# A fused attention and feed-forward kernel: new due times, filler transposes, batch 1's q on GpSimd, a halved last step

## The chip, the cores and the metric

The kernel runs on one core of a Trainium2 chip. The metric is the device time of one execution in microseconds (us), measured on the chip; each time below is a median of several runs, or the time of one profiled run where that is said.

The engines are named as the profile names them: PE (TensorE, matrix products and transposes), PEld (its weight loads), DVE (VectorE), ACT (ScalarE), POOL (GpSimd) and SP (SyncE, which only issues transfers here).

## The reference

```python
def _attn_ref(q, k, v):                       # each 8 batches x 8 heads x 576 x 64
    q_s = q - np.max(q, axis=-1, keepdims=True)
    q_s = np.exp(q_s)
    q_s = q_s / (np.sum(q_s, axis=-1, keepdims=True) + 1e-09)
    k_s = k - np.max(k, axis=2, keepdims=True)
    k_s = np.exp(k_s)
    k_s = k_s / (np.sum(k_s, axis=2, keepdims=True) + 1e-09)
    kv = np.einsum('bhsd,bhse->bhde', k_s, v)
    return np.einsum('bhsd,bhde->bhse', q_s, kv)

def _moe_ref(x, w_in, w_out, s, b):           # x 4608x512, w_in 512x2048, w_out 2048x512
    h = x @ w_in
    r = np.maximum(h, 0.0)
    g = s * (r * r) + b
    return g @ w_out
```

x is the attention's result, transposed to (batch, position) rows by (head, d) columns. All data are float32. To keep float32's accuracy on PE's faster fp32r products, every factor of the two large products is split in a high and a low part, and each product is three matmuls: high by high, high by low, low by high.

## The kernel before

**Blocks and steps.** The 4608 rows of x are done in nine blocks of 512: the first 512 positions of each of the eight batches, and a ninth block of the 64 positions that each batch has left. The 2048 columns of w_in are 16 chunks of 128. A step t is one block and one chunk, 144 in all. Step t computes h_t with 12 matmuls (four pieces c of the 512-long contraction, each of three matmuls), each 128x512. ACT takes the relu into r (L751), DVE squares and scales it (L764), ACT adds b and rounds to the high part gh (L766), DVE subtracts to the low part gl (L768). In odd steps of block 0 ACT does the squaring and scaling instead (L755, L757, L759; DVE L761). Then 12 matmuls (four quarters j of three) add g's product with the chunk of w_out into four accumulators acc. h has one PSUM bank, so h_{t+1} can start only when relu_t has read h_t.

**Weights.** In block 0 the chunk f of both weight matrices is loaded (tile st) and split by `conv_w`: ACT L199, L202 and L220, DVE L205, L210, L212, L215 and L222. L222 writes the low part and is the last of a chunk; its result is w_f, which h_f needs.

**Attention.** A unit u is a pair of heads of one batch; a batch has four units, and pr = u // 2 is a pair of units. Batches 0 and 1 (units 0 to 7) go through `q_stream`: maxima of q (L412), subtraction (L414), exp on ACT, sums and reciprocals (L420 to L424), scaling (L426), transposes qT on PE (L430), a copy on ACT (L433), product with kv into xp (L440), and the split of xp in x's high part (ACT L446) and low part (DVE L449). xp of unit u gives piece c = u mod 4 of the block's x: h_0's last piece needs x_0's unit 3, h_16's last piece needs unit 7. `k_stream`, `k_pair`, `kv_stream` and `kv_second` make kv for these batches. In the later batches (`k_late`, `q_late`, `kv_late`, `x_late`) q's subtraction and scaling are on POOL (L575, L592), and x comes from xp and xq (L676) by way of a tile y (ACT L682, DVE L686).

**The end.** `leave` copies a finished accumulator out and stores it; `leave_last` does so for the last block. There quarters 0 and 1 are copied by ACT, quarter 2 by DVE, and quarter 3 by both, half each; each quarter is stored by two transfers, one from SP's queue and one from ACT's.

**What sets the order.** Nothing reorders at compile time: each engine runs its instructions in the order in which a planner, the class `Order`, writes them. Each stream (one unit's q, one chunk's conversion, one step ...) is a generator that yields an `Op(engine, cost, due, needs ...)` ahead of each piece of work. The planner takes, over and over, the piece that can start first by its own costs, and among those that start within NEAR of it the one with the smallest due. Due times are written by hand: the tables DUE_K, DUE_Q, DUE_V (by unit or pair) and DUE_W, and t - 1, t - 2 and t + 0.5 in the steps. TRIP and RATE are its estimate of a transfer, COLD the time until which it counts PE at half speed. In `needs`, a piece names what has to be there first; `late` adds a margin.

Of the kernel before, what the change touches and what calls it, by code (L numbers as in the profile page):

```python
# [26 lines left out]
def attention_moe(ctx: ExitStack, tc: tile.TileContext, q, k, v, w_in, w_out, s, b, out):  # L27
# [375 lines left out]
    def q_stream(u):  # L403
# [10 lines left out]
        nc.vector.tensor_tensor(out=qt, in0=qt, in1=bc(qm, [P, 2, NT, D]), op=ALU.subtract)  # L414
# [11 lines left out]
        nc.vector.tensor_tensor(out=qe, in0=qe, in1=bc(qr, [P, NT, 2, D]), op=ALU.mult)  # L426
# [231 lines left out]
    def x_late(u):  # L658
# [19 lines left out]
        for a, at in enumerate((slice(0, L), slice(L, L + M))):  # L678
            for h in range(2):
                yield Op("ACT", 0.4, due, take=() if y else ["tmp"])  # L680
                y = y or work.tile([P, 2 * L], F32, name=f"y_{u}", tag="tmp", bufs=NTMP)
                nc.scalar.copy(y[half[h], at], parts[h][a][half[1 - h]])  # L682
        for a, at in enumerate((slice(0, L), slice(L, L + M))):
            for h in range(2):
                yield Op("DVE", 0.44, due, free=["big", "sm"] if a and h else ())
# [52 lines left out]
    def step(t):  # L738
# [12 lines left out]
        nc.scalar.activation(r, hp_, AF.Relu)  # L751
# [31 lines left out]
    def o_parts(t):  # L783
# [4 lines left out]
        for j in tile_order(t):  # L788
# [3 lines left out]
            for i, (g, w_) in enumerate(((gh, w[:, 0]), (gh, w[:, 1]), (gl, w[:, 0]))):  # L792
                nc.tensor.matmul(  # L793
                    acc[blk, j // 2][:, j % 2], g[:, js], w_, start=(f == 0 and i == 0), stop=(f == NFC - 1 and i == 2)
                )
            yield
# [14 lines left out]
    def leave_last(j):  # L811

        t = NSTEP - 1

        whole, half = slice(0, DO), (slice(0, DO // 2), slice(DO // 2, DO))
        todo = [("ACT", 0.55, whole), ("ACT", 0.55, whole), ("DVE", 0.6, whole), ("ACT", 0.35, half[0])][j]
        yield Op(todo[0], todo[1], t, needs=[f"o{t} {j}"])
        a = acc[B, j // 2][:, j % 2]
        if not lasts:
            lasts.append(work.tile([P, 2 * NT * P], F32, name="last", tag="qhl"))  # L820
        o = work.tile([P, DO], F32, name=f"o_{B}_{j}", tag="qe", bufs=2) if j > 1 else lasts[0][:, j * DO:(j + 1) * DO]
        (nc.vector.tensor_copy if j == 2 else nc.scalar.copy)(o[:, todo[2]], a[:, todo[2]])  # L822
        if j == NQ - 1:
            yield Op("DVE", 0.4, t, needs=[f"o{t} {j}"])
            nc.vector.tensor_copy(o[:, half[1]], a[:, half[1]])
        for i, (e, eng) in enumerate((("SP", nc.sync), ("ACT", nc.scalar))):
            yield Op(e, 0.1, t)
            bb = 2 * j + i
            eng.dma_start(out[bb * S + TB:(bb + 1) * S, :], o[i * LEFT:(i + 1) * LEFT, :])
# [130 lines left out]
```

## Time and profile before

| | us |
|---|---|
| median of 3 runs | 875.56 |
| lowest, highest | 875.45, 876.37 |
| profiled run, its own time | 875.49 |
| span of the profile | 873.7 |
| PE busy | 850.2 |
| DVE busy | 573.0 |
| ACT busy | 411.2 |
| POOL busy | 96.0 |
| mean granted PE clock | 0.995 |

The span begins with the first instruction that the profiler shows and ends with the last; 1.8 us of the run's time lie around it. Busy times are sums over instructions, so an engine's share of the span is an average over stages in which different engines set the pace. A row of the timeline gives start, duration, engine, line, operation, result and operands; what stands in brackets behind it is the engine's idle time just before it and what ended that.

### The profile page before, as it was taken

How to read it: one execution, taken by the hardware profiler on the slowest of the kernel's cores; microseconds unless marked ns; L12 is line 12 of the kernel's file. 1: busy time of each engine (PE TensorE's matmuls, PEld its weight loads, DVE VectorE, ACT ScalarE, POOL GpSimd, SP SyncE). 2: the span in 40 equal slices, each digit the busy share in tenths (PEclk: the TensorE clock that was granted, in tenths of full speed). 3: DMA queues.
4: the chain of work that ended last, by engine and by line, in shares of the span. 5: the costliest groups of instructions: out<-in, count | busy, mean ns of one | idle time of the engine just before them, and what ended most of it. 6: DMA issues, size and time to landing. Idle time of an engine off the chain costs nothing.

```text
span 873.7 us, 11481 instructions
## 1 busy us (share of the span) xinstructions
PE 850.2 (97%) x4312; PEld 698.1 (80%) x4312; DVE 573.0 (66%) x931; ACT 411.2 (47%) x676; POOL 96.0 (11%) x110
## 2 busy tenths in 40 slices
PE   4799999999999999999999999999999999999997
PEld 3577887888888888888888888888888888888886
DVE  6999997687887957696577748685764322232222
ACT  5898854455453544454345534444444322222222
POOL 1000002020221201220031102020200010000000
PEclk9999999999999999999999999999999999999999
DMA  9968024524444224332433242431411000000001
GB/s 241 314 249 266 6 73 117 140 80 90 135 107 128 57 73 116 111 74 64 129 88 86 84 130 72 99 88 71 98 50 51 25 25 1 0 28 22 1 0 49
DMA packets 109959, 79.44 MB, mean 91 GB/s; under 512 B 60624, under 2 KB 103632, under 8 KB 109776
## 3 DMA queue, kind: packets, MB, share of 16 engines
q1 hardware_dynamic: 108496, 77.60, 31.9%
q10 hardware_dynamic: 1408, 1.12, 0.4%
q8 instruction: 34, 0.56, 0.3%
q14 instruction: 21, 0.17, 0.1%
HBM read 60.29 MB, written 18.40 MB: 90 GB/s over the span
## 4 chain that ended last, share of the span: by engine, by line
PE 85%; DVE 5%; DMA 3%; issue 3%; ACT 2%; SPq 2%; ACTq 0%; DVEq 0%
PE h L726 41%; PE acc L793 40%; PE kv L298 2%; DMA v<-in_v_dram 1%; DMA st<-in_moe_w_out_dram 1%; DVE low L215 1%; PE xq L676 1%; PE xp L676 1%; DVE w L222 1%; DMA k<-in_k_dram 1%; DVE st L212 1%; DVE st L210 0%; DVE low L205 0%; ACT r L751 0%; PE xp L440 0%
## 5 line engine op out<-in xcount | busy, mean ns | idle before, releaser
L726 PE MATMUL h<-x,w 128*128 128x512 f32 x1728 | 421.6, 392 | 2.6 <-DVE x L449 1.0
L726 PEld LDWEIGHTS h<-x,w 128*128 128x128 f32 x1728 | 323.8, 188 | 72.2 <-DVE x L449 1.7
L793 PE MATMUL acc<-w,gh 128*128 128x512 f32 x1152 | 358.1, 392 | 0.0
L793 PEld LDWEIGHTS acc<-w,gh 128*128 128x128 f32 x1152 | 214.1, 188 | 44.6 <-ACT last L822 0.4
L764 DVE SCALAR_TENSOR_TENSOR r<-r,sb 128x512 f32<-128x512 f32 x136 | 107.7, 792 | 199.0 <-ACT r L751 198.1
L793 PE MATMUL acc<-w,gl 128*128 128x512 f32 x576 | 224.8, 390 | 0.3 <-DVE gl L768 0.3
L751 ACT ACTIVATE r<-h 128x512 f32<-128x512 f32 x144 | 85.9, 597 | 280.5 <-PE h L726 277.1
L768 DVE SCALAR_TENSOR_TENSOR gl<-r,sb,gh 128x512 fp32r<-128x512 f32 x136 | 105.0, 772 | 54.1 <-ACT gh L766 53.3
L766 ACT ACTIVATE gh<-r,sb 128x512 fp32r<-128x512 f32 x136 | 98.5, 724 | 80.5 <-DVE r L764 79.5
L793 PEld LDWEIGHTS acc<-w,gl 128*128 128x128 f32 x576 | 108.1, 188 | 24.2 <-DVE gl L768 0.9
L575 POOL TENSOR_TENSOR q<-q,qm 128x640 f32<-128x640 f32 x24 | 35.4, 1486 | 163.3 <-DVE qm L573 163.3
L592 POOL TENSOR_TENSOR qe<-qe,qr 128x640 f32<-128x640 f32 x24 | 36.6, 1527 | 45.4 <-DVE qr L588 34.7
L682 ACT COPY y<-xp 64x320 f32<-64x320 f32 x48 | 20.2, 420 | 11.7 <-PE xp L676 11.1
L298 PEld LDWEIGHTS kv<-v,k 128*64 128x64 f32 x600 | 19.8, 143 | 7.3 <-issue 4.9
L656 POOL TENSOR_TENSOR spare<-kvf,spare 128x256 fp32r<-128x256 f32 x12 | 9.3, 778 | 144.9 <-issue 137.8
L686 DVE TENSOR_TENSOR y<-xp,y 64x320 f32<-64x320 f32 x48 | 23.4, 488 | 1.4
L613 DVE TENSOR_TENSOR qhl<-qT,qhl 64x640 fp32r<-64x640 f32 x24 | 20.6, 860 | 5.2 <-ACT qhl L608 4.6
L298 PE MATMUL kv<-v,k 128*64 128x65 f32 (+1 forms) x600 | 21.9, 230 | 2.1 <-DMA v<-in_v_dram 2.1
L579 ACT ACTIVATE qe<-q 128x640 f32<-128x640 f32 x24 | 18.8, 786 | 9.1 <-POOL q L575 9.1
L690 ACT CAST x<-y 128x512 fp32r<-128x512 f32 x24 | 14.7, 614 | 15.5 <-DVE y L686 15.5
L686 DVE TENSOR_TENSOR y<-xq,y 64x256 f32<-64x256 f32 x48 | 20.2, 422 | 1.4
L562 ACT ACTIVATE k<-k 128x640 f32<-128x640 f32 x24 | 17.4, 736 | 7.3 <-DVE k L524 7.3
(121 smaller groups left out, 608.5 us busy)
## 6 DMA issues: line engine op xcount, KB each, us to landing
st<-in_moe_w_in_dram SPq DMA_DIRECT2D x16, 512.0 KB, 8.6
st<-in_moe_w_out_dram SPq DMA_DIRECT2D x16, 512.0 KB, 8.6
out_dram<-o SPq DMA_DIRECT2D x16, 512.0 KB, 2.6
turned<-q SPq DMA_DIRECT2D x24, 320.0 KB, 2.3
qT<-turned SPq DMA_DIRECT2D x48, 160.0 KB, 3.1
q<-in_q_dram SPq DMA_DIRECT2D x14, 512.0 KB, 5.3
k<-in_k_dram SPq DMA_DIRECT2D x14, 512.0 KB, 4.3
v<-in_v_dram SPq DMA_DIRECT2D x56, 128.0 KB, 4.8
```

The source lines that it names most:

```text
L298: nc.tensor.matmul(kv[h * D:(h + 1) * D, i], kt[:, i, h, n], vt[:, 2 * i + h, n], start=(n == 0), stop=(n == NT - 1))
L575: nc.gpsimd.tensor_tensor(out=qt, in0=qt, in1=bc(qm, [P, 2, NT, D]), op=ALU.subtract)
L592: nc.gpsimd.tensor_tensor(out=qe_, in0=qe_, in1=qr, op=ALU.mult)
L613: nc.vector.tensor_tensor(out=t[half[1 - h], h], in0=qT[half[h]], in1=t[half[h], h].bitcast(F32), op=ALU.subtract)
L682: nc.scalar.copy(y[half[h], at], parts[h][a][half[1 - h]])
L686: nc.vector.tensor_tensor(out=y[half[h], at], in0=parts[h][a][half[h]], in1=y[half[h], at], op=ALU.add)
L726: nc.tensor.matmul(hp_, w[:, j, c, :], x[:, c, :], start=(c == 0 and i == 0), stop=(c == NP - 1 and i == 2))
L751: nc.scalar.activation(r, hp_, AF.Relu)
L764: nc.vector.scalar_tensor_tensor(out=r, in0=r, scalar=s_col, in1=r, op0=ALU.mult, op1=ALU.mult)
L766: nc.scalar.activation(gh, r, AF.Identity, bias=b_col)
L768: nc.vector.scalar_tensor_tensor(out=gl, in0=r, scalar=b_col, in1=gh.bitcast(F32), op0=ALU.add, op1=ALU.subtract)
L793: nc.tensor.matmul(acc[blk, j // 2][:, j % 2], g[:, js], w_, start=(f == 0 and i == 0), stop=(f == NFC - 1 and i == 2))
```

## The change

Five things change.

1. All due times of batches 0 and 1 and of the first weight chunk, and the planner's constants (a transfer's TRIP 3.0 and RATE 0.315, COLD 8, PE's first piece at 3.0), and the costs that it counts for two pieces of `k_pair` and for v's load.
2. Fillers: up to h_0, where the planner sees PE idle, it puts transposes of the identity into a tile `unused` that nobody reads, which has h's bank: 26, 10, 2, 11, 10, 1 and 5 of them, 65 in all.
3. In units 4 to 7 (batch 1) the subtraction of q's maxima (L414) and the scaling (L426) go from DVE to POOL.
4. In `x_late`, the second unit of a pair also needs y of the first, with the margin WAIT; the two copies (and the two additions) to a half of y are one piece to the planner.
5. In the last step (t = 143) relu, r, gh and gl work in halves of 256 columns; the last quarter's product is two halves of three matmuls, and each half is copied and stored by itself, in four transfers in place of two.

```diff
-    DUE_K = (-30, 0.5, -20, -25, 3.5, 11.5, 12, 19.5)
-    DUE_Q = (-18, -32.5, -13.5, -6, 12.5, 9, -30.5, 64.5)
-    DUE_V = (-81.5, -28.5, -14, 31)
-    DUE_W = -15
+    DUE_K = (-41.5, -21, -37, -39.5, 4.5, 4, 12, 73.5)
+    DUE_Q = (-3.5, -35.5, -27, -7, 12.5, 3.5, -39, 78)
+    DUE_V = (-37, -28, 1.5, 15)
+    DUE_W = -28
...
-        NEAR, HOP, TRIP, RATE = 0.1, 0.15, 2.8, 0.33
-        COLD = 18
+        NEAR, HOP, TRIP, RATE = 0.1, 0.15, 3.0, 0.315
+        COLD = 8
...
+                if eng == "PE":
+
+                    self.idle(t - self.at[eng], "h" in o.take)
...
-        yield Op("DVE", 0.73, due)
-        nc.vector.tensor_tensor(out=qt, in0=qt, in1=bc(qm, [P, 2, NT, D]), op=ALU.subtract)
+        eng, cost, e = ("DVE", 0.73, nc.vector) if bb == 0 else ("POOL", 1.4, nc.gpsimd)
+        yield Op(eng, cost, due)
+        e.tensor_tensor(out=qt, in0=qt, in1=bc(qm, [P, 2, NT, D]), op=ALU.subtract)
...
-        yield Op("DVE", 0.73, due)
-        nc.vector.tensor_tensor(out=qe, in0=qe, in1=bc(qr, [P, NT, 2, D]), op=ALU.mult)
+        yield Op(eng, cost, due)
+        e.tensor_tensor(out=qe, in0=qe, in1=bc(qr, [P, NT, 2, D]), op=ALU.mult)
...
-            "PE", 0.57, due - NFC, needs=[f"q{u}", f"kvhl{pr}", f"h{NFC * (bb - 1) - 1}"], take=["big", "sm"],
+            "PE", 0.57, due - NFC, needs=[f"q{u}", f"kvhl{pr}", f"h{NFC * (bb - 1) - 1}"] + [f"y{u - 1}"] * i, take=["big", "sm"],
...
+        if t == NSTEP - 1:
+
+            halves = [slice(i * TB // 2, (i + 1) * TB // 2) for i in range(2)]
+            for i, c in enumerate(halves):
+                if i:
+                    yield Op("ACT", 0.35, t - 2, free=["h"])
+                nc.scalar.activation(r[:, c], hp_[:, c], AF.Relu)
...
+            for c in [slice(i * DO // 2, (i + 1) * DO // 2) for i in range(2)] if t == NSTEP - 1 and j == NQ - 1 else [slice(0, DO)]:
+                for i, (g, w_) in enumerate(((gh, w[:, 0]), (gh, w[:, 1]), (gl, w[:, 0]))):
+                    nc.tensor.matmul(
+                        acc[blk, j // 2][:, j % 2, c], g[:, js], w_[:, c], start=(f == 0 and i == 0),
+                        stop=(f == NFC - 1 and i == 2 and c.stop == DO)
+                    )
...
+        parts = half_ if j == NQ - 1 else [whole]
+        for k, c in enumerate(parts):
+            dve = j == 2 or k
+            yield Op("DVE" if dve else "ACT", 0.6 / len(parts), t, needs=[f"o{t} {j + k}"])
...
+            for i, (e, eng) in enumerate((("SP", nc.sync), ("ACT", nc.scalar))):
+                yield Op(e, 0.1, t)
+                bb = 2 * j + i
+                eng.dma_start(out[bb * S + TB:(bb + 1) * S, c], o[half[i], c])
...
+    unused = [ps.tile([P, 512], F32, name="unused", tag="h")]
+
+    def idle(us, last):
+        if last:
+            unused.clear()
+        for _ in range(int(0.6 * us / 0.109) if unused else 0):
+            nc.tensor.transpose(unused[0][:, 0:P], ident, ident)
```

The line numbers of the changed kernel are higher: by 3 up to `kv_stream`, by 5 from q's subtraction on, by 23 to 31 in the steps and stores.

How the order moves, at three places. In these rows stand the line, the operation, result and operands with their tile numbers, and the shape; h_16 is step 16's h, x_1 the second block's x, acc_0_0 and acc_0_2 block 0's accumulators of quarters 0, 1 and 2, 3.

PE from h_15 to h_17, before:

```order
L726 MATMUL h_15_1259<-x_0_288,w_15_1230 128x512 x12
L430 MATMUL qT_7_1279<-ident_78,qe_7_1249 128x128 x5
L726 MATMUL h_16_1290<-x_1_948,w_0_231 128x512 x9
L440 MATMUL xp_7_1306<-early_85,kvf1_84 128x256
L440 MATMUL xp_7_1306<-early_85,kvf1_84 128x320
L793 MATMUL acc_0_0_467<-w_15_1230,gh_15_1286 128x512 x2
L793 MATMUL acc_0_0_467<-w_15_1230,gl_15_1287 128x512
...
L726 MATMUL h_16_1290<-x_1_948,w_0_231 128x512 x3
L793 MATMUL acc_0_2_482<-w_15_1230,gh_15_1286 128x512 x2
L793 MATMUL acc_0_2_482<-w_15_1230,gl_15_1287 128x512
...
L726 MATMUL h_17_1347<-x_1_948,w_1_431 128x512 x12
```

The same place after the change, from the last of step 15's products:

```order
L824 MATMUL acc_0_2_549<-w_15_1257,gh_15_1300 128x512 x2
L824 MATMUL acc_0_2_549<-w_15_1257,gl_15_1301 128x512
L731 MATMUL h_16_1330<-x_1_865,w_0_277 128x512 x3
L435 MATMUL qT_7_1379<-ident_78,qe_7_1235 128x128 x5
L445 MATMUL xp_7_1388<-early_85,kvf1_84 128x256
L445 MATMUL xp_7_1388<-early_85,kvf1_84 128x320
L731 MATMUL h_16_1330<-x_1_865,w_0_277 128x512 x3
L731 MATMUL h_17_1410<-x_1_865,w_1_493 128x512 x12
```

Before, step 15's twelve products stand between xp_7 and h_17; after, they all stand ahead of qT_7, and qT_7, xp_7, the last piece of h_16 and h_17 follow each other directly. Between h_15 and these rows now stand half of step 14's products, kv_3, nine matmuls of h_16, xp_6 and step 15's products.

DVE just ahead of w_15, the last conversion (low0_15 and st_15 are its operands; q0 is batch 1's raw q, qm_7 unit 7's maxima, qe_6 unit 6's exp), before:

```order
L768 SCALAR_TENSOR_TENSOR gl_14_1159<-r_14_1157,sb_90,gh_14_1158 128x512
L426 TENSOR_TENSOR qe_6_1162<-qe_6_1162,qr_6_1182 128x640
L215 ISA low0_15_991<-st_15_883,low0_15_991 128x2048
L304 TENSOR_SCALAR z_3_1219<-kv_3_1188 128x2
L305 RECIPROCAL z_3_1219<-z_3_1219 128x2
L307 TENSOR_TENSOR zr_3_1222<-own_86,z_3_1219 128x4
L412 TENSOR_REDUCE qm_7_1228<-q0_93 128x10
L313 TENSOR_TENSOR kvf1_84<-kv_3_1188,zr_3_1222 128x256
L414 TENSOR_TENSOR q0_93<-q0_93,qm_7_1228 128x640
L222 TENSOR_TENSOR w_15_1230<-low0_15_991,w_15_1230 128x2x512
```

After, on DVE, at the same place:

```order
L425 TENSOR_REDUCE qs_6_1229<-qe_6_1220 128x10
L790 SCALAR_TENSOR_TENSOR r_14_1231<-r_14_1231,sb_90 128x512
L427 TENSOR_SCALAR qs_6_1229<-qs_6_1229 128x10
L429 RECIPROCAL qr_6_1245<-qs_6_1229 128x10
L218 ISA low0_15_1066<-st_15_965,low0_15_1066 128x2048
L794 SCALAR_TENSOR_TENSOR gl_14_1233<-r_14_1231,sb_90,gh_14_1232 128x512
L454 TENSOR_TENSOR x_1_865<-xp_4_1226,x_1_865 128x512
L225 TENSOR_TENSOR w_15_1257<-low0_15_1066,w_15_1257 128x2x512
```

And on POOL, all of batch 1's q after the change, with k's memsets between; before, POOL has only these memsets there:

```order
L419 TENSOR_TENSOR q0_93<-q0_93,qm_5_463 128x640
L431 TENSOR_TENSOR qe_5_507<-qe_5_507,qr_5_660 128x640
L490 MEMSET k0_92 64x2x64 x2
L419 TENSOR_TENSOR q0_93<-q0_93,qm_4_1105 128x640
L490 MEMSET k0_92 64x2x64 x2
L431 TENSOR_TENSOR qe_4_1128<-qe_4_1128,qr_4_1184 128x640
L419 TENSOR_TENSOR q0_93<-q0_93,qm_6_1189 128x640
L419 TENSOR_TENSOR q0_93<-q0_93,qm_7_1203 128x640
L431 TENSOR_TENSOR qe_6_1220<-qe_6_1220,qr_6_1245 128x640
L431 TENSOR_TENSOR qe_7_1235<-qe_7_1235,qr_7_1284 128x640
```

The scaling of unit 6, unit 7's subtraction and kv_3's four rows are gone from DVE ahead of w_15; on POOL stand four subtractions and, ahead of w_15, three scalings (that of unit 7 comes after it).

PE at steps 31 to 33, after the change:

```order
L731 MATMUL h_32_2182<-x_2_1749,w_0_277 128x512 x9
L824 MATMUL acc_1_0_1432<-w_15_1257,gh_31_2163 128x512 x2
L824 MATMUL acc_1_0_1432<-w_15_1257,gl_31_2164 128x512
L824 MATMUL acc_1_0_1432<-w_15_1257,gh_31_2163 128x512 x2
L824 MATMUL acc_1_0_1432<-w_15_1257,gl_31_2164 128x512
L824 MATMUL acc_1_2_1451<-w_15_1257,gh_31_2163 128x512 x2
L824 MATMUL acc_1_2_1451<-w_15_1257,gl_31_2164 128x512
L824 MATMUL acc_1_2_1451<-w_15_1257,gh_31_2163 128x512 x2
L824 MATMUL acc_1_2_1451<-w_15_1257,gl_31_2164 128x512
L731 MATMUL h_32_2182<-x_2_1749,w_0_277 128x512 x3
L731 MATMUL h_33_2240<-x_2_1749,w_1_493 128x512 x12
```

Before, all twelve matmuls of h_32 stand ahead of step 31's products; now three of them stand behind, next to h_33.

More of the change, by code (lines that the diff above doesn't have):

```diff
@@ L357, in sm @@
             return ps.tile([P, 512], F32, name=f"{n}_{pr}", tag="sm", bufs=1)
-        yield Op("DVE", 1.13, due, needs=[f"k{u} there" for u in us])
+        yield Op("DVE", 0.69, due, needs=[f"k{u} there" for u in us])
         kt = by_head(tiles[pr][0])
@@ L678, in x_late @@
         for a, at in enumerate((slice(0, L), slice(L, L + M))):
+            yield Op("ACT", (0.84, 0.74)[a], due, take=() if a else ["tmp"])
+            y = y or work.tile([P, 2 * L], F32, name=f"y_{u}", tag="tmp", bufs=NTMP)
             for h in range(2):
[L680 to L681 removed]
                 nc.scalar.copy(y[half[h], at], parts[h][a][half[1 - h]])
         for a, at in enumerate((slice(0, L), slice(L, L + M))):
+            yield Op("DVE", (0.98, 0.84)[a], due, free=["big", "sm"] if a else (), gives=[f"y{u}"] if a else ())
             for h in range(2):
[L685 removed]
                 nc.vector.tensor_tensor(out=y[half[h], at], in0=parts[h][a][half[h]], in1=y[half[h], at], op=ALU.add)
@@ L777, in step @@
             next(parts)
+            if t == NSTEP - 1 and j == NQ - 1:
+                yield Op("PE", 0.36, t + 0.5, gives=[f"o{t} {NQ}"])
+                next(parts)
     def tile_order(t):
@@ L791, in o_parts @@
             js = slice(j * P, (j + 1) * P)
[L792 to L796, printed above, removed]
+            for c in [slice(i * DO // 2, (i + 1) * DO // 2) for i in range(2)] if t == NSTEP - 1 and j == NQ - 1 else [slice(0, DO)]:
[3 more added lines that the diff above has]
+                        stop=(f == NFC - 1 and i == 2 and c.stop == DO)
+                    )
+                yield
     def leave(blk, j):
@@ L813, in leave_last @@
         t = NSTEP - 1
[L815 to L829, printed above, removed]
+        whole, half_ = slice(0, DO), (slice(0, DO // 2), slice(DO // 2, DO))
+        o = None
+        parts = half_ if j == NQ - 1 else [whole]
+        for k, c in enumerate(parts):
+            dve = j == 2 or k
+            yield Op("DVE" if dve else "ACT", 0.6 / len(parts), t, needs=[f"o{t} {j + k}"])
+            a = acc[B, j // 2][:, j % 2]
+            if not lasts:
+                lasts.append(work.tile([P, 2 * NT * P], F32, name="last", tag="qhl"))
+            if o is None:
+                o = work.tile([P, DO], F32, name=f"o_{B}_{j}", tag="qe", bufs=2) if j > 1 else lasts[0][:, j * DO:(j + 1) * DO]
+            (nc.vector.tensor_copy if dve else nc.scalar.copy)(o[:, c], a[:, c])
+            for i, (e, eng) in enumerate((("SP", nc.sync), ("ACT", nc.scalar))):
+                yield Op(e, 0.1, t)
+                bb = 2 * j + i
+                eng.dma_start(out[bb * S + TB:(bb + 1) * S, c], o[half[i], c])
     NU = B * NP
@@ L884, in v_ @@
         def v_():
-            yield Op("SP", 3.2, due, needs=[f"kv{p}"], gives=[f"v{pr} there"], kb=864)
+            yield Op("SP", 3.2, due, needs=[f"kv{p}"], gives=[f"v{pr} there"], kb=1100)
             load_v(pr)
```

29 lines of the change are left out of this document (21 added, 8 removed).

## The prediction

> **What bounds the kernel now.** I read the busy times first, then the windows by stage (in the window rows: stretch, length, busy time and instructions of PE, PEld, DVE, ACT and POOL, granted clock, DMA share, GB/s), then the waits.
>
> ```profile
> PE 850.2 (97%) x4312; PEld 698.1 (80%) x4312; DVE 573.0 (66%) x931; ACT 411.2 (47%) x676; POOL 96.0 (11%) x110
> 0.00:38.70 38.70, 21.58 (x169) 16.86 (x169) 31.51 (x60) 27.16 (x50) 2.97 (x18) 0.96 1.00 282
> 45.60:130.30 84.70, 83.90 (x442) 67.31 (x441) 83.86 (x123) 69.34 (x91) 1.50 (x4) 1.00 0.44 143
> 130.30:140.70 10.40, 10.20 (x46) 7.97 (x45) 6.38 (x13) 5.50 (x11) 0.00 (x0) 1.00 0.47 114
> 140.70:860.00 719.30, 718.65 (x3601) 594.07 (x3601) 442.30 (x725) 301.33 (x516) 91.55 (x88) 1.00 0.27 73
> PE xq L676 <- DVE y L686: 0.7, 3, 0.2
> ```
>
> From 140.7 us to 860 PE is busy in all but 0.65 us, and 0.7 is what the chain of waits of its three xq stops sums to. Nothing can be won there but that. So the kernel's time is the start of h_17 (140.74) plus a fixed rest, and what counts is everything before h_17. In 45.6 to 130.3 DVE is as full as PE (83.86 of 84.70): the weight conversions and batch 1's q share it.
>
> ```profile
> 45.57 1.23 DVE L222 TENSOR_TENSOR w<-low,w 128x1024 fp32r<-128x1024 f32 x1 [1.08 <-ACT w L220]
> 22.75 0.76 DVE L336 TENSOR_REDUCE km<-kT 128x1 f32<-128x576 f32 x1 [0.31 <-PE kT L333]
> 124.90 0.82 DVE L426 TENSOR_TENSOR qe<-qe,qr 128x640 f32<-128x640 f32 x1
> 126.77 0.15 DVE L304 TENSOR_SCALAR z<-kv 128x2 f32<-128x2 f32 x1
> 127.24 0.81 DVE L412 TENSOR_REDUCE qm<-q 128x10 f32<-128x640 f32 x1
> 127.97 0.41 DVE L313 TENSOR_TENSOR kvf<-kv,zr 128x256 f32<-128x256 f32 x1
> 128.30 0.82 DVE L414 TENSOR_TENSOR q<-q,qm 128x640 f32<-128x640 f32 x1
> 129.03 1.22 DVE L222 TENSOR_TENSOR w<-low,w 128x1024 fp32r<-128x1024 f32 x1
> 130.30 2.91 PE L726 MATMUL h<-x,w 128*128 128x512 f32 x12
> 140.74 2.88 PE L726 MATMUL h<-x,w 128*128 128x512 f32 x12
> ```
>
> The last conversion, w_15, ends at 130.25, and h_15 starts at 130.30: there PE and DVE arrive together.
>
> **DVE up to w_15.** Seven q operations on its path (four subtractions, three scalings) go to POOL. From start to start they take 0.73 (128.30 to 129.03): 5.1. kv_3's operations move behind w_15: 126.77 to 127.24 and 127.97 to 128.30, 0.8. The 0.31 of idle before km goes, since kT now stands earlier, and of the 1.08 I count half, 0.5, as ACT still makes that operand. Without any other effect w_15 would end at 130.25 - 6.7 = 123.5.
>
> **What POOL takes back.** The same subtraction and scaling already run on POOL for later batches, and the rows beside them show the price:
>
> ```profile
> 296.00 0.75 DVE L764 SCALAR_TENSOR_TENSOR r<-r,sb 128x512 f32<-128x512 f32 x1
> 475.93 1.26 POOL L575 TENSOR_TENSOR q<-q,qm 128x640 f32<-128x640 f32 x1 [12.79 <-DVE qm L573]
> 475.93 1.81 DVE L764 SCALAR_TENSOR_TENSOR r<-r,sb 128x512 f32<-128x512 f32 x1
> 388.98 1.27 POOL L592 TENSOR_TENSOR qe<-qe,qr 128x640 f32<-128x640 f32 x1 [1.07 <-DVE qr L588]
> 388.77 0.82 DVE L582 TENSOR_REDUCE qs<-qe 128x20 f32<-128x640 f32 x1
> L222 DVE TENSOR_TENSOR w<-low,w 128x1024 fp32r<-128x1024 f32 x14 | 17.2, 1226 | 1.5 <-ACT w L220 1.5
> L210 DVE TENSOR_SCALAR st<-st 128x1024 f32<-128x1024 f32 x12 | 8.2, 693 | 0.0
> ```
>
> A DVE operation of two SBUF inputs that starts with a POOL one takes 1.81 where 0.75 is normal, 1.06 more, nearly all of POOL's 1.26; a reduction (one input) keeps its 0.82. Between 45 and 129 us DVE is full, so each block counts. No row has a tensor_scalar beside a POOL tensor_tensor, and half of a conversion is such. L210 moves 1024 columns in 0.693 where two-input L222 needs 1.226, so it moves twice as much per time; I take it as blocked too, by that likeness. In the order, four of the seven POOL operations meet such work soon after they can start (1.06 each); three start beside a reduction of 0.8 first (1.26 - 0.8 = 0.45): 4 x 1.06 + 3 x 0.45 = 5.6. Ends: 0, since the waits of POOL for DVE may put them beside reductions and PSUM readers alone, and 7 x 1.26 = 8.8. If only two-input operations block, 3.8. With 5.6 w_15 ends at 129.1 and h_15 starts there. On POOL itself the seven take 1.26 each out of 85 us; k's memsets (L485) stand in the same queue, so a scaling that waits for DVE's sums holds a memset back, and kv_3 waits for that, which costs nothing while kv_3 stands behind h_15. ACT's exp of these units waits for 1.26 in place of 0.73, with several steps to spare before their qT. The Trainium skill (SBUF — State Buffer, Who interferes with whom) calls this an exclusive lock on a port pair that DVE shares with GpSimd, held for the whole instruction; it spares reductions, as the trace does (0.82). It says that a tensor_scalar contends only where it enters a two-port mode, which no run here shows; by the other reading the time would be that of 3.8, 878.8.
>
> **Is PE ready earlier?** h_0 waits for x3's parts on DVE:
>
> ```profile
> 35.77 0.83 DVE L420 TENSOR_REDUCE qs<-qe 128x10 f32<-128x640 f32 x1
> 37.26 0.73 PE L726 MATMUL h<-x,w 128*128 128x512 f32 x2 [1.04 <-DVE x L449]
> 38.67 3.68 PE L726 MATMUL h<-x,w 128*128 128x512 f32 x8 [0.69 <-ACT r L751]
> PE h L726 <- ACT r L751: 0.9, 2, 0.7
> 35.37:38.78 3.41, 1.47 (x5) 1.00 1.05 219
> 38.78:42.20 3.42, 3.42 (x9) 0.50 0.92 237
> 124.63 1.39 PE L298 MATMUL kv<-v,k 128*64 128x65 f32 x40
> 40.24 0.51 SPq L183 DMA_DIRECT2D st<-in_moe_w_in_dram  x1
> 41.50 0.43 SPq L183 DMA_DIRECT2D st<-in_moe_w_in_dram  x1
> ```
>
> q_5's subtraction (0.82 as L414) and sums (0.83, with 0.15 of small ones) stand before x3 now and not after: h_0 1.8 earlier. Up to h_15 PE also loses kv_3 (1.32 to the next start), xp_6 (1.0) and half of o_14 (six matmuls of 0.227, 1.36), which go behind it: 3.7. So PE alone would be at h_15 by 130.30 - 1.8 - 3.7 = 124.8; DVE at 129.1 is later and decides. The fillers, 65 transposes of an unused tile before h_0, buy only clock: after the stretch with 1.47 busy (43%) comes one at 0.50, whose 3.42 us do 1.71 of work. They end at h_0, the waits around h_0 and h_1 stay, and this window with them; ends: 1.7 gained (124.8 becomes 123.1), or nothing. Both lie under DVE's 129.1. On SP's queue q's reload moves behind one more weight; in this stretch the DMA engines are full (1.05, 0.92), and the loads they bring are wanted only when DVE, the later one, comes to them. One weight takes 1.3 of the queue (40.24 to 41.50), so the ends are 1.3 lost by q and 1.3 gained by that weight; I take nothing, as both lie under DVE's lateness; a late one would show as ACT waiting for w's load.
>
> **Step 16.** In the new order qT_7, xp_7 and the last quarter of h_16 stand in a row on PE, with o_15 used up before them.
>
> ```profile
> 118.85 0.77 PE L430 MATMUL qT<-ident,qe 128*128 128x128 f32 x5
> 119.65 0.64 ACT L433 COPY early<-qT 128x576 f32<-128x576 f32 x1 [0.41 <-PE qT L430]
> 136.14 1.13 PE L440 MATMUL xp<-early,kvf 128*128 128x256 f32 x4
> 137.31 0.59 ACT L446 CAST x<-xp 128x512 fp32r<-128x512 f32 x1 [0.85 <-PE xp L440]
> 138.04 0.69 DVE L449 TENSOR_TENSOR x<-xp,x 128x512 fp32r<-128x512 f32 x1 [0.51 <-ACT xleft L240]
> ```
>
> qT_7 to xp_7: 118.85 to 120.29 and a hop, 1.48. xp_7 to the last quarter: 136.14 to 138.73, 2.6; that quarter 0.68; then h_17 needs the only h bank, so relu_16: 0.69 as at h_1. Together 3.95. From h_15 to h_17: h_15 2.72, six of o_14 1.36, kv_3 1.32, six of h_16 1.36, three of o_15 0.68, xp_6 1.0, nine of o_15 2.04, three of h_16 0.68, then 1.48 and 3.95: 16.6. Before it was 140.74 - 130.30 = 10.44. Only 3.7 of the 6.2 more is moved work; 2.5 is new idle. h_17 comes at 129.1 + 16.6 = 145.7, 5.0 later.
>
> **Later.** Before h_33 three matmuls of h_32 now stand last, behind all of o_31, so its relu is exposed as at h_1: PE waited 0.69 there, and with the hand-over lost 0.86. The second unit of an x pair asks for y of the first: the three xq stops (0.7) should go; what stands behind the waiting xp on PE is only what the order put there, and PE has other rows first. The two copies, and the two additions, of a unit that the planner now takes as one are as many as before: 0. Ends: 0.7 gained, 0.7 lost again.
>
> **The tail.**
>
> ```profile
> 869.10 0.47 ACTq L829 DMA_DIRECT2D out_dram<-last  x1
> 869.42 0.42 DVE L825 COPY o<-acc 128x256 f32<-128x256 f32 x1 [1.52 <-ACT o L822]
> 869.87 0.50 ACTq L829 DMA_DIRECT2D out_dram<-o  x1
> ```
>
> The halves of step 143 end a wait of 0.1 for gl. The two last half copies are already halves before; the change lets ACT's start after the first half's matmuls, but ACT then issues one store more (0.5) before the last one. For the stores I take 0, ends -0.4 and +0.4; the 0.1 counts.
>
> **Sum.** 5.0 + 0.9 - 0.7 - 0.1 = 5.1. The profiled run took 875.49 (span 873.7), the median is 875.56, so the two agree within 0.1: 880.6.
>
> **Rivals.**
> - A, the forecast: DVE pays for POOL's port and step 16 lies open. With 3.8 to 8.8 for the port, 878.8 to 883.8.
> - A2: PE's new idle of 2 to 3 us before h_15 and in step 16 each leaves a stretch like 35.37 to 38.78, and the next runs at 0.50: 1.7 more for each, 882.3 to 884. For it speaks that row, against it that 1.47 of 3.41 busy may be just at the edge. The Trainium skill (TensorE: Matmul & The Clock Gate, What's actually happening) speaks of a wholly idle window before the clock falls; by that A2 wouldn't occur, while the row above shows a fall after 43%.
> - B, no measurable change: POOL's operations fall beside reductions and cost about nothing. h_15 comes when PE is ready, 123.5 to 124.8, h_17 at 140.1 to 141.4: with 0.2 from later, 875.0 to 876.4. The exposed 2.5 of step 16 eats what x3 and q give. For it: what is left of q on DVE is reductions (0.81 each), which aren't blocked. Against it: the 1.81 beside 1.26, and the conversions, which fill the rest of DVE.
> - C, faster: the fillers keep the clock up through h_1, so PE arrives at h_15 by 123.1, and DVE, unblocked, loses all of the 1.08 too (122.9). h_17 then at 139.7, 874.6; it is over 0.2% (1.75 us, about what a measurement of this kernel can tell) only if step 16 is 0.8 shorter than 16.6, so h_17 before 138.8: 873.7. Against it: the parts of 3.95 (1.13, 0.59, 0.69, 0.68) leave 0.3 to save.
> - D, the change does not do what it says: fillers and halves alone move nothing, since h_0 waits for DVE and the stores for their queue; the rest is then as in A or B.
>
> **How the numbers follow.** A 0.60, A2 0.10, B 0.20, C 0.10. A and A2 are slower (0.70), B the same, C faster. The time is A's, whose own range is 878 to 883. B's low end and A2's high end leave out less than 2 in 10: 874.6 to 884.0.
>
> **What would show it.** In the changed kernel: POOL rows of the new subtraction and scaling between 40 and 130 us with two-input DVE rows beside them at 1.7 or more; PE idle before h_15, released by DVE's w; near h_17 three waits in a row (xp for ACT's early, h for DVE's x, h for ACT's r), 2.5 together; a second wait of h for r of 0.7 near h_33; no xq wait; the last store's issue as far from the last matmul as before. The forecast is wrong if those DVE rows keep 0.75 and 1.23, or if h_15 starts before 127.

## The result and the profile after

The changed kernel takes 884.02 us (median of 4 runs, 883.73 to 885.29) against 875.50 for the kernel before on the same chip: a ratio of 1.0096, 95% interval 1.0081 to 1.0111, 8.5 us slower. The forecast was 880.6, with 874.6 to 884.0 as its range, so the result lies at the range's upper end. The profiled run is the longest of the four (885.29, span 883.4); the two traces differ by 9.7.

The page's busy times, and four windows of the changed kernel cut at the same places of the program as those of before (up to h_1, up to h_15, up to h_17, up to the end):

```profile
PE 859.9 (97%) x4380; PEld 705.2 (80%) x4380; DVE 572.3 (65%) x925; ACT 413.2 (47%) x678; POOL 105.3 (12%) x118
0.00:38.36 38.36, 27.96 (x234) 22.64 (x234) 30.35 (x58) 26.44 (x49) 4.56 (x19) 1.00 0.95 286
45.60:131.06 85.46, 80.84 (x386) 63.76 (x384) 84.09 (x115) 67.09 (x88) 12.97 (x10) 0.99 0.41 135
131.06:148.61 17.55, 15.12 (x97) 11.23 (x95) 5.44 (x12) 6.31 (x11) 1.26 (x1) 0.97 0.64 164
148.61:868.00 719.39, 718.06 (x3592) 593.87 (x3593) 440.79 (x725) 302.39 (x515) 86.55 (x88) 1.00 0.26 71
```

Before, the stretch up to h_15 had 0.8 us of PE idle; now it has 4.6. DVE is still full there (84.09 of 85.46), although seven operations left it. From h_15 to h_17 it is 17.55, where it was 10.44. What follows has 1.3 of idle, before 0.65.

Where the difference arose is seen best from the start of each step's relu (ACT r from h), in us against the kernel before, in the profiled runs of this document. Steps 14 to 17 and 31 to 34 are the places of the order that move; old_fill and old_tail, left out here, stay within 0.5 of the kernel before at all of them:

| step | changed | q_on_dve | cover16 | cover16_kv3 | kv3_q_dve | no_fill | old_q_pool | old_xmargin | best_parts |
|---|---|---|---|---|---|---|---|---|---|
| 0 | -0.3 | -1.0 | -1.4 | -1.1 | -1.2 | +1.4 | +0.1 | +1.2 | -0.1 |
| 2 | -1.7 | -2.4 | -2.8 | -2.4 | -2.6 | +1.2 | -1.0 | 0.0 | -1.3 |
| 14 | +0.9 | -1.0 | +1.1 | +2.8 | +0.9 | +5.2 | +1.5 | 0.0 | -1.2 |
| 15 | +1.2 | -1.5 | -1.5 | -0.4 | -1.0 | +2.4 | +1.5 | 0.0 | -1.2 |
| 17 | +9.6 | +6.9 | +4.8 | +7.0 | +5.5 | +10.8 | +2.0 | 0.0 | -1.3 |
| 31 | +9.6 | +6.9 | +4.1 | +6.9 | +5.4 | +10.8 | +2.0 | -0.1 | -1.2 |
| 34 | +10.2 | +7.5 | +8.9 | +7.0 | +5.5 | +11.4 | +2.0 | +0.8 | -1.2 |
| 48 | +11.6 | +9.0 | +10.3 | +6.9 | +5.3 | +12.8 | +2.0 | +0.6 | -1.3 |
| 142 | +9.9 | +7.2 | +8.5 | +5.1 | +3.5 | +11.0 | +2.0 | -1.2 | -3.1 |

So in the changed kernel 1.2 is lost up to step 15 and 8.4 from there to step 17; of these 8.4, 3.7 is work that was moved behind h_15. From step 17 to step 142 only 0.3 is added, but that is a balance: 2.0 is lost from step 31 to step 48 and 1.8 won after. (At step 34 the loss looks smaller, +10.2, because 40 matmuls of a kv product, 1.3 us, then still lie ahead that in the kernel before lie behind.)

**POOL beside DVE.** The timeline of the changed kernel, DVE and POOL, where batch 1's last units are worked on:

```profile
106.81 3.37 POOL L419 TENSOR_TENSOR q<-q,qm 128x640 f32<-128x640 f32 x1 [33.42 <-ACT w L223]
107.19 1.21 DVE L225 TENSOR_TENSOR w<-low,w 128x1024 fp32r<-128x1024 f32 x1
108.32 0.74 DVE L790 SCALAR_TENSOR_TENSOR r<-r,sb 128x512 f32<-128x512 f32 x1
117.91 1.69 POOL L431 TENSOR_TENSOR qe<-qe,qr 128x640 f32<-128x640 f32 x1
119.56 3.38 POOL L419 TENSOR_TENSOR q<-q,qm 128x640 f32<-128x640 f32 x2
120.06 1.75 DVE L787 TENSOR_TENSOR gl<-r,gh 128x512 fp32r<-128x512 f32 x1
121.73 1.75 DVE L215 TENSOR_SCALAR st<-st 128x1024 uint32<-128x1024 uint32 x1
123.40 0.81 DVE L425 TENSOR_REDUCE qs<-qe 128x10 f32<-128x640 f32 x1
125.34 2.05 POOL L431 TENSOR_TENSOR qe<-qe,qr 128x640 f32<-128x640 f32 x1 [2.41 <-DVE qr L429]
126.20 1.75 DVE L794 SCALAR_TENSOR_TENSOR gl<-r,sb,gh 128x512 fp32r<-128x512 f32 x1
128.47 1.21 DVE L225 TENSOR_TENSOR w<-low,w 128x1024 fp32r<-128x1024 f32 x1
```

Two-input operations at 120.06 and 126.20 take 1.75, and so does a tensor_scalar (0.69 without POOL, 1.75 at 121.73): both are blocked, as taken. The reduction keeps 0.81. Summed over the DVE rows beside POOL's from 45 us to w_15 the lengthening is 5.3. POOL pays too: unit 4's subtraction takes 3.37 where the shortest such row took 1.26, while w at 107.19 and r at 108.32, two-input rows beside it, keep their time. So sometimes the one waits and sometimes the other.

**PE at steps 14 to 17.** The timeline of PE in the changed kernel, the rows with a wait in brackets and some without:

```profile
119.64 0.76 PE L435 MATMUL qT<-ident,qe 128*128 128x128 f32 x5 [1.59 <-POOL qe L431]
128.00 0.50 PE L824 MATMUL acc<-w,gl 128*128 128x512 f32 x1 [1.59 <-DVE gl L794]
131.06 3.43 PE L731 MATMUL h<-x,w 128*128 128x512 f32 x12
144.44 1.24 PE L445 MATMUL xp<-early,kvf 128*128 128x256 f32 x4 [0.73 <-ACT early L438]
146.35 0.49 PE L731 MATMUL h<-x,w 128*128 128x512 f32 x1 [0.68 <-ACT x L451]
147.19 0.73 PE L731 MATMUL h<-x,w 128*128 128x512 f32 x2 [0.34 <-DVE x L454]
148.61 1.60 PE L731 MATMUL h<-x,w 128*128 128x512 f32 x4 [0.69 <-ACT r L775]
243.31 0.73 PE L731 MATMUL h<-x,w 128*128 128x512 f32 x2 [0.56 <-DVE x L699]
244.79 3.01 PE L731 MATMUL h<-x,w 128*128 128x512 f32 x12 [0.75 <-ACT r L775]
```

PE waits 1.59 for POOL's late scaling of unit 4, then 1.59 for gl_14, which took 1.75 in place of 0.75 beside unit 6's scaling (126.20 above). Then come the three bare waits of step 16 (for the copy of qT, for x in two rows, for the relu), 2.4 together, and the two at h_32 and h_33.

**The clock.** Windows of PE alone (length, busy time, granted clock, DMA share, GB/s):

```profile
9.24:12.65 3.41, 1.53 (x12) 1.00 1.13 338
12.65:16.07 3.42, 2.27 (x19) 1.00 0.71 176
118.50:121.91 3.41, 2.27 (x13) 1.00 0.00 0
125.32:128.74 3.42, 1.46 (x5) 1.00 0.06 14
128.74:132.15 3.41, 3.41 (x11) 0.50 0.01 2
142.39:145.80 3.41, 2.56 (x13) 1.00 1.33 232
145.80:149.22 3.42, 1.84 (x6) 1.00 0.77 290
149.22:152.63 3.41, 3.41 (x10) 0.50 0.08 4
```

A stretch with 1.46 busy and one with 1.84 were each followed by a stretch at 0.50 (a half-rate stretch below), worth 1.7 us, half of 3.41; 2.27 and 2.56 were not. In the traces of this document, the tail left out, every full-clock stretch with at most 1.92 busy (the highest: no_fill, 37.16 to 40.58) was followed by a half-rate one, but for the first row here, and none with 1.94 or more (the lowest: cover16, 9.75 to 13.16). The half-rate stretch near 40 us that the kernel before has is gone here; best_parts below shows that this need not be the change's doing.

### The profile page after: what moved, and what is told of

Read it like the earlier page. It is cut to its first block, busy times and chain, and to the rows that moved or that the text cites. A ratio compares the mean times of both kernels' runs of the same rounds, so it can differ in the third digit from the quotient of the medians.

```text
span 883.4 us, 11647 instructions
## 1 busy us (share of the span) xinstructions
PE 859.9 (97%) x4380; PEld 705.2 (80%) x4380; DVE 572.3 (65%) x925; ACT 413.2 (47%) x678; POOL 105.3 (12%) x118
## 4 chain that ended last, share of the span: by engine, by line
PE 83%; DVE 3%; ACT 1%; issue 0%; ACTq 0%
PE h L731 40%; PE acc L824 40%; PE kv L301 2%; PE xp L681 1%; PE xq L681 1%; DVE r L790 0%; DVE gl L794 0%; DVE low L218 0%; PE xp L445 0%; PE qT L435 0%; DVE y L691 0%; ACT r L775 0%; DVE gl L787 0%; DVE st L215 0%; DVE k L482 0%
## 5 line engine op out<-in xcount | busy, mean ns | idle before, releaser
L597 POOL TENSOR_TENSOR qe<-qe,qr 128x640 f32<-128x640 f32 x24 | 31.9, 1329 | 60.6 <-DVE qr L593 40.7
L687 ACT COPY y<-xp 64x320 f32<-64x320 f32 x48 | 20.2, 421 | 17.0 <-PE xp L681 16.6
L567 ACT ACTIVATE k<-k 128x640 f32<-128x640 f32 x24 | 17.6, 738 | 16.6 <-DVE k L529 14.8
L601 DVE STREAM_TRANSPOSE q<-qe 128x640 f32<-128x640 f32 x24 | 19.9, 830 | 6.2 <-POOL qe L597 6.2
L661 POOL TENSOR_TENSOR spare<-kvf,spare 128x256 fp32r<-128x256 f32 x12 | 10.2, 850 | 114.4 <-issue 87.1
L202 ACT ACTIVATE low<-st 128x1024 int32<-128x1024 uint32 (+1 forms) x17 | 18.7, 1102 | 4.8 <-DVE w L225 3.5
```

The lines of the kernel that those rows point to most:

```text
L597: nc.gpsimd.tensor_tensor(out=qe_, in0=qe_, in1=qr, op=ALU.mult)
L601: nc.vector.transpose(out=tb, in_=qe.rearrange("p h t n r -> p (h t n r)"))
```

## The experiments

Each was timed in five rounds beside the kernel before; its own times on those chips were 875.4 to 875.9. 95% intervals are those of the ratio.

**q_on_dve: the order kept, q back on DVE.**

```diff
-        eng, cost, e = ("DVE", 0.73, nc.vector) if bb == 0 else ("POOL", 1.4, nc.gpsimd)
+        eng, cost, e = ("DVE", 0.73, nc.vector) if bb == 0 else ("POOL", 1.4, nc.vector)
```

> The changed kernel with the order on every engine kept, but the eight q operations of batch 1 issued on DVE again, at the places that they had on POOL. Theory (POOL gives DVE nothing: in the changed kernel DVE rows beside the POOL ones are longer by 5.3 us in all, as much as 7 x 0.73 = 5.1 saved, and the chain through POOL makes PE wait 1.6 for qT_4 and 1.6 for gl_14 and brings a half-rate window): w_15 ends within 0.5 us of 129.7, the two PE waits go, h_15 starts about 1.4 earlier than 131.1, and the time is 1 to 3 us under the changed kernel. Rival (POOL relieves DVE, the loss is all from the order): 4 to 5 us slower than the changed kernel.

882.75, ratio 1.0076 (1.0063 to 1.0089): 1.3 under the changed kernel's median, 2.5 under it in the profiled runs. w_15 did not stay within 0.5 of 129.7, it ended 2.5 earlier, at 127.19, and h_15 began 2.5 earlier, at 128.52 (its relu 2.7: -1.5 for +1.2). PE no longer waits for POOL, but it still waits for step 14's g (the first row is w_15):

```profile
125.98 1.22 DVE L225 TENSOR_TENSOR w<-low,w 128x1024 fp32r<-128x1024 f32 x1
PE acc L824 <- DVE gl L794: 1.3, 1, 1.3
PE acc L824 <- ACT gh L792: 0.9, 1, 0.9
```

So POOL is worth nothing to this kernel, or a little less: the two intervals overlap, so the 1.3 is not certain. With q on DVE it is still 6.9 over the kernel before, so most of the 8.5 us come from the rest of the change, its order above all. The half-rate stretch around the start of h_15 stayed (125.97 to 129.38), which the expectation did not have.

**old_q_pool: the order of before, q on POOL.** In the kernel before, the two q lines issue on POOL for batch 1, and the planner is told nothing:

```diff
-        nc.vector.tensor_tensor(out=qt, in0=qt, in1=bc(qm, [P, 2, NT, D]), op=ALU.subtract)
+        (nc.gpsimd if bb else nc.vector).tensor_tensor(out=qt, in0=qt, in1=bc(qm, [P, 2, NT, D]), op=ALU.subtract)
...
-        nc.vector.tensor_tensor(out=qe, in0=qe, in1=bc(qr, [P, NT, 2, D]), op=ALU.mult)
+        (nc.gpsimd if bb else nc.vector).tensor_tensor(out=qe, in0=qe, in1=bc(qr, [P, NT, 2, D]), op=ALU.mult)
```

> The kernel before, with nothing changed but the engine of the eight q operations of batch 1: POOL in place of DVE, the order of every engine kept. Theory (each POOL operation blocks DVE by up to 1.06 us, and DVE's stream blocks POOL, so its results come later): 0 to 3 us slower than before, DVE rows of 1.7 beside the POOL ones. Rival (POOL is worth the 5.1 us that it takes from DVE, PE then being the limit with 0.8 of idle): 0.5 to 0.8 us faster.

878.04, ratio 1.0027 (1.0017 to 1.0037), 2.2 slower. DVE rows beside POOL's are longer here as well (w at 129.93 takes 2.07 for 1.22), and PE waits 1.0 and 0.75 for POOL's scalings. In this run the stretch near 40 us was at full clock, without a filler, so it led by 1.0 at step 2; by step 15 it was 1.5 behind. So in the old order the move loses for certain, and in the new one it gains nothing.

**cover16: step 15's products spread over step 16's waits.** A name is given by each transposition and each xp, and step 15's quarters ask for those of unit 7:

```diff
-                "PE", 0.68, t + 0.5, needs=[f"w{t} 1"] * first + [f"o{t - 1} {j}"] * (t > 0),
+                "PE", 0.68, t + 0.5, needs=[f"w{t} 1"] * first + [f"o{t - 1} {j}"] * (t > 0) + ([[], ["qT 7"], ["xp 7"], ["xp 7"]][j] if t == 15 else []),
```

> The changed kernel with step 15's products held back on PE: its second quarter waits in the planner for qT_7, its third and fourth for xp_7, so that they lie between qT_7, xp_7 and the last piece of h_16. Theory (the three bare waits of step 16, 0.73 + 1.02 + 0.69, and the half-rate window after them cost what they show): waits fall from 2.4 to about 1.1 and the window at 0.50 near 150 us goes, 1.3 to 3 us faster than the changed kernel. Rival (the loss is made before h_15 and step 16 only passes it on): within 0.5.

885.81 (884.03 to 886.08), ratio 1.0112 (1.0098 to 1.0126): no gain, so neither reading fits the time. In the profiled run step 17 stands at +4.8, 4.8 us earlier than in the changed kernel. But 2.7 of these stand at step 15 already (-1.5 for +1.2), ahead of the edit: up to there PE, DVE, ACT and POOL run the same rows in the same order. What differs is where the half-rate stretch fell, ten us earlier than in the changed kernel's profiled run, where PE could still catch up, since h_15 has to wait for w_15 anyway:

```profile
118.97:122.39 3.42, 3.42 (x12) 0.50 0.00 0
127.40 1.21 DVE L225 TENSOR_TENSOR w<-low,w 128x1024 fp32r<-128x1024 f32 x1
128.90 2.91 PE L731 MATMUL h<-x,w 128*128 128x512 f32 x12
```

The edit's own share is 2.1: the waits of step 16 fell from 2.4 to 1.7, and h_17 is at full clock. So step 16 gave about what the theory said. But between steps 31 and 34 all of the 4.8 but 1.3 was lost again, at h_32's x:

```profile
239.08 0.49 PE L731 MATMUL h<-x,w 128*128 128x512 f32 x1 [1.37 <-ACT x L695]
240.41 0.73 PE L731 MATMUL h<-x,w 128*128 128x512 f32 x2 [0.84 <-DVE x L699]
241.88 4.58 PE L731 MATMUL h<-x,w 128*128 128x512 f32 x12 [0.75 <-ACT r L775]
```

These waits sum to 3.0, and the twelve matmuls behind them take 4.58 for 2.9, a half-rate stretch. The profiled run is the shortest of the four, at least 1.7 under the others, and that of the changed kernel the longest of its four, which flatters this comparison. Something else held x_2 back: the transfers of batch 2's k. SP's queue, the kernel before, and then the changed one:

```profile
125.94 0.37 SPq L277 DMA_DIRECT2D k<-in_k_dram  x1
```

```profile
137.09 0.37 SPq L280 DMA_DIRECT2D k<-in_k_dram  x1
```

They start 1.3 after kv_3 (124.63 before, 135.78 after; in cover16 134.41 after 133.10), which reads the buffer that they fill. kv_3 was moved behind h_15; I had counted that as a gain of 1.3 and 0.8.

**cover16_kv3: kv_3 ahead of h_15 again**, on top of cover16.

```diff
-    DUE_V = (-37, -28, 1.5, 15)
+    DUE_V = (-37, -28, 1.5, 13)
```

> The kernel of cover16 with one number more changed: DUE_V of pair 3 from 15 to 13, which puts kv_3 before h_15 on PE again. Theory (what was lost again at step 32 comes from kv_3: the loads of batch 2's k and v wait for it and began at 137.1 in place of 125.9, so x_2 was late): these loads start by 123, h_32 and h_33 wait for nothing, the half-rate window near 244 goes, and the time is 5 to 8 us under the changed kernel, 876 to 879. Rival (x_2 is late because its second unit asks for y of the first with a margin): h_32 still waits 1 to 2 us for x, 882 to 885.

880.38 (880.21 to 881.05), ratio 1.0060 (1.0047 to 1.0074): 5.4 under cover16 and 3.6 under the changed kernel. The loads start at 117.91, from step 31 to 48 nothing is lost (+6.9, +6.9), PE has no recorded wait after 150 us, and the rival is out: the need for y is unchanged here. It fell short of 876 to 879, as step 16 now waits 2.7 for x on DVE. Batch 2's q, which now comes earlier too, is in the way: on DVE its sums, which waited for an exp, and a copy of a finished accumulator stand ahead of x from 139.97 on, and x's other operand was there by 140.5. The two stretches behind this wait (143.15 to 149.97) ran at half rate.

```profile
140.71 1.22 DVE L836 COPY o<-acc 128x1024 f32<-128x1024 f32 x1
142.98 0.68 DVE L454 TENSOR_TENSOR x<-xp,x 128x512 fp32r<-128x512 f32 x1
143.71 1.22 PE L731 MATMUL h<-x,w 128*128 128x512 f32 x2 [2.73 <-DVE x L454]
```

**kv3_q_dve: the same with q on DVE.**

```diff
-        eng, cost, e = ("DVE", 0.73, nc.vector) if bb == 0 else ("POOL", 1.4, nc.gpsimd)
+        eng, cost, e = ("DVE", 0.73, nc.vector) if bb == 0 else ("POOL", 1.4, nc.vector)
...
-    DUE_V = (-37, -28, 1.5, 15)
+    DUE_V = (-37, -28, 1.5, 13)
```

> The kernel of cover16_kv3 with batch 1's q issued on DVE at its places in the order. Theory (POOL's port and the late results cost more than DVE saves, in any order): the waits of PE for DVE's x (2.7) and for POOL's q (1.0) shrink, 1 to 3 us under cover16_kv3, 877.4 to 879.4; what is left over the kernel before is the order. Rival (with kv_3's work back ahead of h_15, DVE has no room and needs POOL): 1 to 4 us over cover16_kv3.

880.72 (878.95 to 881.51), ratio 1.0052 (1.0040 to 1.0065): in the medians the same as cover16_kv3, in the profiled runs 1.4 less. The wait of 2.7 for x stayed (2.67), POOL's 1.0 went and 1.8 for DVE's x came before qT. Neither reading is borne out; with kv_3 early the engine of q matters less than the noise.

**no_fill: the changed kernel without fillers.**

```diff
-        for _ in range(int(0.6 * us / 0.109) if unused else 0):
+        for _ in range(int(0.6 * us / 0.109) if False else 0):
```

> The changed kernel without its 65 filler transposes, all else kept. Theory (the fillers keep the clock up in the stretch after h_0, but DVE sets h_15): the window at 0.50 near 40 us is back, h_2 starts 1.7 later, by step 7 nothing of it is left, and the time is within 0.5 us of the changed kernel. Rival (the fillers are worth their window at the end): 1.7 slower.

886.46, ratio 1.0127 (1.0113 to 1.0141): 2.4 slower than with fillers in the medians, 1.0 in the profiled runs. My theory fell. h_0's relu itself comes 1.7 later, and PE's waits for ACT ahead of it show why: the transposes that feed ACT run slower.

```profile
PE kn L349 <- ACT early L344: 6.5, 3, 2.7
```

This wait is 3.9 with fillers; without them the five transposes of a kT still take 1.27 at 17.46, with them 0.75 at 6.97. The half-rate stretch near 41 us is back, and the two behind it, 122.50 and 149.81, are there with fillers too (128.71 and 149.19).

**old_fill: fillers on the kernel before.** The hook and the unused tile alone, 48 transposes by its own planner.

```diff
+                if eng == "PE":
+                    self.idle(t - self.at.get(eng, 3.0), "h" in o.take)
...
+        for _ in range(int(0.6 * us / 0.109) if unused else 0):
+            nc.tensor.transpose(unused[0][:, 0:P], ident, ident)
```

> The kernel before with fillers alone (48 transposes, where its own planner sees PE idle up to h_0; the order is kept otherwise). Theory (without fillers the changed kernel's h_0 came 1.7 later, by slow transposes ahead of it and a window at 0.50 behind; the kernel before has both): h_2 starts 1.5 to 2.5 earlier, DVE then sets h_15, which can gain 0.3 to 1.1, the idle time that is left to it: 0.3 to 1.1 us faster. Rival (the kernel's rate up to h_15 is DVE's alone): within 0.2.

874.49 (873.80 to 875.72), ratio 0.9992 (0.9983 to 1.0001). Not to be told from nothing with certainty; if it is a gain, it is 0.7. In the profiled run h_2 starts only 0.3 earlier, not 1.5 to 2.5: the half-rate stretch near 40 us is still there (39.08 to 42.49), behind one with 1.74 busy.

**old_xmargin: the need for y on the kernel before.**

```diff
-needs=[f"q{u}", f"kvhl{pr}", f"h{NFC * (bb - 1) - 1}"], take=["big", "sm"],
+needs=[f"q{u}", f"kvhl{pr}", f"h{NFC * (bb - 1) - 1}"] + [f"y{u - 1}"] * i, take=["big", "sm"],
```

> The kernel before with the need of the second unit for y of the first alone, with its margin. Theory (the three xq waits of 0.22 go and nothing else moves by more than a place): 0.4 to 0.7 us faster. Rival (the later second unit makes x late at the next block): h of the next block waits for x, 0.5 to 2 us slower.

874.41 (873.40 to 874.67), ratio 0.9988 (0.9979 to 0.9998): 1.0 faster. Both readings hold in part: 0.9 is lost between steps 31 and 34, and 2.0 is won after (+0.8 to -1.2). In the kernel before, the three recorded stops stood at 0.22 each; here the two products lie between matmuls of h and follow each other without a stop. The first two rows are the kernel before, the others this run:

```profile
384.90 0.31 PE L676 MATMUL xp<-spare 128*128 128x320 f32 x1
385.43 0.36 PE L676 MATMUL xq<-spare 128*128 128x256 f32 x1 [0.22 <-DVE y L686]
386.78 0.31 PE L676 MATMUL xp<-spare 128*128 128x320 f32 x1
386.93 0.28 PE L676 MATMUL xq<-spare 128*128 128x256 f32 x1
```

They cost about 0.6 each, nearly three times what is recorded. From start to start it is 0.53 with the stop and 0.15 without: the record counts idle time only from the modelled end of xp, 0.31 after its start, and so leaves out 0.16.

**old_tail: the last step in halves on the kernel before.**

```diff
-        nc.scalar.activation(r, hp_, AF.Relu)
...
+                nc.scalar.activation(r[:, c], hp_[:, c], AF.Relu)
...
+                eng.dma_start(out[bb * S + TB:(bb + 1) * S, c], o[half[i], c])
```

> The kernel before with the last step in halves alone. Theory (the wait of 0.1 for gl goes, the stores end where they did): 0 to 0.3 us faster. Rival (the stores of the first half leave earlier and the end comes with them): 0.4 to 0.8 faster; or, by one more issue on ACT's queue: 0.3 slower.

875.09, ratio 0.9998 (0.9989 to 1.0007): no change that can be seen.

**best_parts.** The kernel before with the fillers, the halves, and the need for y from block 3 on:

```diff
-needs=[f"q{u}", f"kvhl{pr}", f"h{NFC * (bb - 1) - 1}"], take=["big", "sm"],
+needs=[f"q{u}", f"kvhl{pr}", f"h{NFC * (bb - 1) - 1}"] + [f"y{u - 1}"] * (i and bb > 2), take=["big", "sm"],
```

> The kernel before, with its own due times and q on DVE, plus the parts of the change that did no harm alone: fillers, the last step in halves, and the second unit's need for y of the first, this from block 3 on only (in block 2 it made h_32 wait). Theory (the three xq waits cost 0.57 each at the next steps, not 0.22, and block 2's wait took 0.8 of the gain): 1.7 to 2 from x, 0.3 to 1 from fillers, 0 to 0.3 from the end: 2 to 3.3 us under the kernel before. Rival (the gain is as small as the recorded waits, 0.7): 0.7 to 1.2 under it.

872.45 (871.57 to 873.48), ratio 0.9964 (0.9951 to 0.9978): 3.3 us faster than the kernel before and 11.6 faster than the changed one. Nothing is lost at step 32 now (-1.2 at 31 and at 34), and 1.9 is won after it. The profiled run has no half-rate stretch between 21 us and its last microsecond. Below are h_1, then the two stretches around it in old_fill, and the same two in best_parts:

```profile
38.53 3.01 PE L728 MATMUL h<-x,w 128*128 128x512 f32 x12 [0.69 <-ACT r L772]
35.66:39.08 3.42, 1.74 (x6) 1.00 1.11 222
39.08:42.49 3.41, 3.41 (x10) 0.50 0.85 205
36.49:39.90 3.41, 2.10 (x8) 1.00 0.99 175
39.90:43.31 3.41, 3.41 (x17) 1.00 0.93 237
```

h_1's twelve matmuls take 3.01 here; before, eight of them took 3.68. The waits ahead of them are as before (1.0 for x, 0.69 for the relu). It is not the fillers that keep the clock there: old_fill has the same ones, and its PE runs the same rows in the same order up to 255 us, and yet it has the half-rate stretch; old_q_pool and old_xmargin have no filler and don't have it. What differs is where the waits fall among the stretches, so that 1.74 of one is busy, or 2.10. So of the lead of 1.2 up to step 31 in this trace 1.0 is luck; the 1.9 after it is the need for y. The medians hold all the same: all five runs (at most 873.48) are under all nine of the kernel before beside them (at least 874.62).

## Why the prediction was right, and where it was short

The sign and the two main causes held: DVE got nothing from POOL, and step 16 lay bare. The size, 5.1 forecast and 8.5 measured (9.8 in the profiled run), was short. The measured 884.02 lies above A's own range of 878 to 883, at the upper end of A2's: what happened is A with A2's two half-rate stretches, and A2 had been given 0.10. The low end of the whole range, 874.6, is C's figure and not B's (875.0). Term by term, in the profiled run:

- **POOL's port**: 5.6 taken, 5.3 measured on DVE; the tensor_scalar was blocked, as taken by its likeness to a two-fold move. The Trainium skill (SBUF — State Buffer, Who interferes with whom) says that a tensor_scalar can contend; the trace agrees (1.75 for 0.69). What the step left out is the other side: POOL is blocked by DVE as well (3.37 for 1.26), and its results come late. PE waited 1.59 for one and 1.59 for a gl that another had blocked.
- **w_15 at 129.1**: it ended at 129.7, and that it came so near is luck. By q_on_dve the order alone brings w_15 to 127.19, 3.1 earlier than before, where 1.6 was counted (kv_3's operations and two idle times); and with q on POOL it comes 2.5 later than with q on DVE, where the sum had 0.5 (5.6 less 5.1). Two errors cancelled.
- **h_15 = the end of w_15**: failed in this run. With these waits PE fell to a half-rate stretch at 128.74 and began h_15 at 131.06, 1.4 after w_15. In cover16, with the same order up to there, the stretch came earlier, and h_15 began 0.3 after w_15.
- **x3 1.8 earlier**: failed; 0.3. The sums of q_5 left, but its maxima (0.83 at 32.0) came in their place, and POOL's first subtraction lengthened a conversion ahead of x3 (1.69 for 1.22). It decided nothing: the lead of 1.7 at step 2 is down to 0.1 at step 5.

```profile
32.02 0.83 DVE L415 TENSOR_REDUCE qm<-q 128x10 f32<-128x640 f32 x1
33.95 1.69 DVE L218 CUSTOM_DVE_ANT_0 low<-st,low 128x2048 uint16<-128x2048 uint16 x1
```

- **Step 16**: 16.6 forecast from h_15 to h_17, 17.55 measured. The waits were 2.4 for 2.5; 0.5 of the rest is the end of the half-rate stretch, which runs to 132.15. The next stretch at 0.50, after it, took 1.7 more out of h_17. That an exposed wait brings a half-rate stretch behind it was in A2 and should have been in the sum: after h_0 both stretches with under 1.9 of 3.4 busy had one.
- **Later**: from step 31 to step 48 the changed kernel lost 2.0, 0.9 forecast, with one wait more (x, 0.56). Cause not seen: kv_3's move holds back batch 2's k, costed at nothing; with kv_3 early (cover16_kv3) nothing is lost there.
- **The xq waits**: 0.7 taken, 1.8 won from step 48 to step 142, and about 2 alone. This and the term before it nearly cancel, 0.3 for a forecast of 0.2, so here the sum was right by luck.
- **The fillers**: "buy only clock" at nothing; without them the changed kernel is 2.4 slower. With D's word that they move nothing, this was wrong in the new order; in the old one (old_fill) no gain is certain.
- **The tail**: 0.1 taken, 0.2 gained (from the relu of step 142 to the end it is 15.94 for 16.15); alone it is not to be seen in the medians.

The rivals B and C fell with h_15 at 131.06. What stays open: with kv_3 early and q on DVE the new order is still 5 us slower than the old one. The waits of PE in step 16 and the half-rate stretch behind them are seen there, but no run takes the due times and the planner's constants apart. By the Trainium skill (TensorE: Matmul & The Clock Gate, What's actually happening) the clock falls after an idle window; here it fell after stretches that were 43% and 54% busy, so the measurement decides against the idle window as a condition.
